# Second feed-forward network: an addition moved behind a maximum on the vector engine, and the next activations' load moved ahead of a weight load

## The chip, the cores and the metric

The kernel runs on one core of a Trainium2 chip. A core has a matrix engine (TensorE; PE in the profile, with its weight loads as PEld), a vector engine (VectorE, DVE), a scalar engine (ScalarE, ACT), a general engine (GpSimd, POOL) and a queue that here only issues DMAs (SyncE, SP). The engines run side by side, each in its own program order, and wait for one another by semaphores. The metric is the device time of one execution in microseconds; the profile covers one such execution.

## The reference, cut to what matters

```python
def reference(u, v, z, moe_w_in, moe_w_out, moe2_w_in, moe2_w_out):
    scores = (1 / S) * z @ z.T                       # B = 2, S = 3008, z: 64 wide
    x = u * (np.maximum(scores, 0) ** 2 @ v)         # 6016 tokens, 256 wide
    h = x @ moe_w_in                                 # first network, 256 -> 2048
    x = (h - np.tanh(h)) @ moe_w_out                 # 2048 -> 256
    h = x @ moe2_w_in                                # second network, 256 -> 2048
    g = np.where(h >= 1, h, np.where(h <= -1, 0.0, (h + 1) ** 2 / 4))
    return g @ moe2_w_out                            # 2048 -> 256
```

All is in float32. The kernel splits each operand into a rounded high part and a low rest, and makes a product from three products of such parts.

## The kernel before

The attention comes first and takes about 480 us of the span. Then come the two networks. Tokens are taken in **supertiles** of 1024 (the sixth has 896), the hidden width in 8 slices of 256. One supertile with one slice is a **unit**. The first network has 6 supertiles, so 48 units; the second has 5, so 40 units; its sixth supertile is done by other code at the end (lines 1043 on). Units run one after the other; `f` is the slice, 0 to 7.

A unit (class `Unit`, method `emit`) multiplies activations by input weights in a seven-product scheme for 2 x 2 blocks: `mult` puts three matmuls of 512 columns for each product into one of three PSUM banks, Y, X and V. ScalarE copies banks to SBUF (`snap`: m1, u2, u3), VectorE adds a copy and a bank (`add`). There are two halves, A and B, each of 128 x 1024 values. The first values of half A are m1 + X (in the trace `ha<-m,m`), the second u3 + V (`ha<-u,m`); half B gets a copy (`hb<-m`) and u2 + V (`hb<-u,m`).

Each half of the second network then goes through five steps: `first` clips to -1 and 1 (VectorE, line 519), `square` makes ((t + 1) / 2) squared (ScalarE, line 524), `value` takes the maximum of that and h (VectorE, line 527), `round` makes the high part `gha` or `ghb` (ScalarE, line 501), `rest` makes the low part `gla` or `glb` (VectorE, line 538). The matmuls with the output weights (line 584, `acc<-gha`, `acc<-ghb`, ...) need them. They belong to the unit before, `p`: `emit` interleaves the end of `p` with the start of the present unit. In program order, VectorE does, in a unit of the second network: `first` of p's half B, `rest` of p's half A, the addition m1 + X, `value` of p's half B, one fill, `rest` of p's half B, the addition u3 + V, `first` of half A, one fill, `value` of half A, the addition u2 + V. ScalarE does: m1 copy, `round` of p's A, `square` of p's B, u2 copy, `round` of p's B, the fill's rounding, u3 copy, `square` of A, the copy for half B.

A **fill** is one piece of side work from the list `fills`: preparing the next supertile's activations (`x_steps`, lines 441, 460 and 476), or turning results for output (line 705). A unit takes two. In the second network the units with f = 1 and 2 take four turns, those with f = 3 to 6 the eight preparation steps, and f = 7 and 0 find nothing; in its first supertile there are no turns yet and the preparation lies in f = 2 to 5.

`p.late` is true for every unit of the second network and for the very first unit of the first network, whose first half is rounded one unit later.

The order of the work is the order in which the code is written; no scheduler changes it. All loads go through one queue, SP, which issues in program order and waits at each issue for the buffer's release. `load_w(i + 2)` asks for a unit's weights (three DMAs of 512 KB) two units ahead, into a ring of 24 slots. `load_x` asks for the next supertile's activations (two DMAs of 512 KB into the two buffers `xr`), in the unit with f = 1, behind that unit's weights; the preparation steps are put into `fills` in the unit with f = 2.

Of the kernel before, what the change touches and what calls it, by code (L numbers as in the profile page):

```python
# [29 lines left out]
def attention_then_two_ffn(  # L30
# [60 lines left out]
    def flush():  # L91
        for fn in deferred:
            fn()
        deferred.clear()
# [314 lines left out]
    def load_w(i):  # L409

        if i < len(units):
            net, _, f = units[i]
        else:
            net, f = 1, i - len(units)
            if f >= NPF:
                return
        assert {(net, f, "in"), (net, f, "out")} <= done
        got = []
        for part in range(3):
            w = ring.tile([P, 1024], F32R, tag="w", name=f"w{i}_{part}")  # L420
            nc.sync.dma_start(out=w.bitcast(F32), in_=packed[net, f][:, part, :])
            got.append(w)
        ws[i] = [w.rearrange("p (n f) -> p n f", f=P) for w in got[:2]], got[2].rearrange("p (h j d) -> p h j d", h=2, j=2)
# [67 lines left out]
    def fill():  # L491

        if fills:
            for fn in fills.pop(0):
                if fn is not None:
                    fn()
        else:
            work(CONVERT[1])

    def copy(out_, in_):  # L500
        nc.scalar.activation(out=out_, in_=in_, func=AF.Copy)  # L501

    def add(out_, x, bank):
        nc.vector.tensor_tensor(out=out_, in0=x, in1=bank, op=ALU.add)  # L504
# [46 lines left out]
    class Unit:  # L551
# [59 lines left out]
        def emit(self, p, att=None):  # L611

            w = self.w
            before = p and p.net == 1 and p.f == 0 and p.s and p.before
            self.before = p
            self.late = self.net == 1 or att is not None
            one, two, three = p.parts_list if p else ([], [], [])
            Y = self.bank()
            self.mult(Y, A11, "b11", True)
            m1 = self.snap("m1", Y)  # L620
            if p and p.late:
                p.A.round()
            X = self.bank()
            self.mult(X, A12, "b21", True)
            if p:
                if p.net == 1:
                    p.B.first()
                p.A.rest()
                p.B.first() if p.net == 0 else p.B.square()
            self.A = Half(self.net, w, "a")  # L630
            add(self.A.h[:, 0, :w], m1, X[:, :w])
            V = self.bank()
            self.mult(V, S1, "t1", True)
            self.mult(Y, S2, "t2")
            u2 = self.snap("u2", Y)
            if before:
                before.empty(1)
            if p:
                p.B.value()
            for fn in one[:4] if before else one:  # L640
                fn()
            if att:
                att[0]()
            if p:
                p.B.round()
                fill()
                p.B.rest()
            self.mult(Y, S3, "t3")
            for fn in one[4:] if before else ():
                fn()  # L650
            u3 = self.snap("u3", Y)
            add(self.A.h[:, 1, :w], u3, V[:, :w])
            if self.net == 1 or att:
                self.A.first()
            for fn in two:
                fn()
            if att:
                att[1]()
            if not att:
                fill()  # L660
            if self.net == 1:
                self.A.square()
            self.mult(Y, A22, "t4")
            self.mult(V, S4, "b22")
            self.B = Half(self.net, w, "b")
            if self.net == 0 and not att:
                self.A.first()
            copy(self.B.h[:, 1, :w], Y[:, :w])
            self.A.value()
            if att:  # L670
                flush()
            add(self.B.h[:, 0, :w], u2, V[:, :w])
            for fn in three:
                fn()
            if not self.late:
                self.A.round()
            if p:
                p.empty(0)
            self.parts_list = self.parts()
# [32 lines left out]
    def split_steps():  # L712


        st = {}

        def load():
            for n, size in enumerate(SIZES):
                st[n] = u_p.tile([P, 2, 512], F32, tag="ub", name=f"xe{n}")
                nc.sync.dma_start(out=st[n][:, :, :size], in_=kept[1, LAST][:, :, n * QT : n * QT + size])  # L720

        def hi(n):
            def step():
                xsp[n] = [ring.tile([P, 2, 512], F32R, tag="w", name=f"xe{n}_{i}") for i in range(2)]
                copy(xsp[n][0][:, :, : SIZES[n]], st[n][:, :, : SIZES[n]])

            return step

        def lo(n):
            def step():  # L730
                s = (slice(None), slice(None), slice(0, SIZES[n]))
                nc.vector.tensor_tensor(
                    out=xsp[n][1][s], in0=st[n][s], in1=xsp[n][0].bitcast(F32)[s], op=ALU.subtract
                )

            return step

        return load, [(None, hi(0)), (lo(0), hi(1)), (lo(1), None)]
# [145 lines left out]
    with tc.manual_schedule():  # L884
# [79 lines left out]
        def second(i):  # L964
            if i >= LAG:
                _, av_fn, args = pairs[i - LAG]
                av_fn(*args, *held.pop(i - LAG))
# [50 lines left out]

        p = None
        for i, (net, s, f) in enumerate(units):  # L1020
            if i:
                load_w(i + 2)
            if f == 1:
                more = (net, s + 1) if (net, s + 1, 0) in units else (1, 0) if net == 0 else None
                load_x, steps = x_steps(*more) if more else split_steps()
                load_x()
            elif f == 2:
                fills.extend(steps)
            u = Unit(i)
            u.emit(p, att=(lambda: second(NATT), lambda: second(NATT + 1)) if i == 0 else None)  # L1030
            p = u
# [63 lines left out]
```

## Time and profile before

| What | Before |
|---|---|
| median of 3 runs | 1488.02 us (1487.14 to 1489.27) |
| the profiled execution | 1488.3 us, of which its span 1486.5 us |
| PE busy | 1465.1 us, 99% of the span |
| PEld busy | 1239.5 us, 83% |
| DVE busy | 1270.3 us, 85% |
| ACT busy | 1024.5 us, 69% |
| granted TensorE clock | 0.999 of full speed |

The table is to be read with care: PE's busy time is a modelled one, since matmuls overlap each other, and a share over the whole span mixes the attention with the two networks. The networks have to be looked at by stage and by unit.

### The profile page before, as it was taken

Reading aid. Unit: us, or ns where it says so; the run is one execution under the profiler, and the core shown is the slowest. Engines: PE = TensorE matmul, PEld = TensorE weight load, DVE = VectorE, ACT = ScalarE, POOL = GpSimd, SP = SyncE. Lnnn points to the kernel's source line nnn. Section 1 sums busy time; section 2 is a strip of 40 time slices with the busy share of each in tenths; the row PEclk is TensorE's granted clock in tenths of the full one; section 3 lists DMA queues with packets and bytes.
Section 4 is the critical chain, followed back from the end, with each engine's and each line's share of the span. In section 5 each row is a group of like instructions: output and inputs, shape, how many; then the busy total and the mean of one; then the engine's idle time right before and its main releaser. Section 6 shows DMA issues by size and latency. Waiting matters only on the chain.

```text
span 1486.5 us, 22226 instructions
## 1 busy us (share of the span) xinstructions
PE 1465.1 (99%) x8653; PEld 1239.5 (83%) x8653; DVE 1270.3 (85%) x1511; ACT 1024.5 (69%) x1249; POOL 55.5 (4%) x69
## 2 busy tenths in 40 slices
PE   9999999999999999999999999999999999999998
PEld 6888899999988788888888888977777777777897
DVE  8999888989988789898989888888788888887775
ACT  8877778977777676777666766665666666666543
POOL 0110000000110000000000000000000000000000
PEclk9999999999999999999999999999999999999999
DMA  6333235323345648374665757472564644456361
GB/s 156 87 100 97 82 99 116 79 82 100 100 128 166 228 133 306 138 256 162 234 258 189 275 184 271 154 279 90 176 203 170 198 163 134 150 171 215 128 198 26
DMA packets 202170, 240.81 MB, mean 162 GB/s; under 512 B 130000, under 2 KB 139088, under 8 KB 202064
## 3 DMA queue, kind: packets, MB, share of 16 engines
q1 hardware_dynamic: 200864, 239.12, 49.2%
q8 instruction: 68, 1.11, 0.3%
q10 hardware_dynamic: 1200, 0.26, 0.1%
q14 instruction: 38, 0.31, 0.1%
HBM read 195.69 MB, written 43.65 MB: 161 GB/s over the span
## 4 chain that ended last, share of the span: by engine, by line
PE 79%; DVE 9%; ACT 9%; issue 1%; DMA 1%; SPq 0%; ACTq 0%; DVEq 0%
PE acc L584 24%; PE acc L335 24%; PE m L565 20%; PE sc L287 6%; DVE gla L538 3%; DVE tb L527 3%; PE h L750 3%; ACT ghb L501 3%; ACT gha L501 3%; DVE ha L504 2%; ACT m L501 2%; PE acc L786 1%; PE acc L807 1%; DMA xr<-kept 1%; DVE glb L538 0%
## 5 line engine op out<-in xcount | busy, mean ns | idle before, releaser
L335 PE MATMUL acc<-hi,v 64*128 64x512 f32 (+1 forms) x2256 | 283.8, 383 | 0.0
L335 PEld LDWEIGHTS acc<-hi,v 64*128 64x128 f32 x2256 | 231.3, 184 | 24.0 <-ACT hi L300 0.8
L565 PE MATMUL m<-xht,w 128*128 128x512 f32 (+1 forms) x704 | 215.8, 388 | 0.0
L584 PE MATMUL acc<-ghb,w 128*128 128x512 f32 (+1 forms) x704 | 192.3, 395 | 10.4 <-ACT ghb L501 10.4
L308 ACT ACTIVATE r<-sc 128x1024 f32<-128x1024 f32 (+1 forms) x143 | 143.6, 1004 | 72.1 <-PE sc L287 71.6
L321 DVE TENSOR_TENSOR lo<-a,hi 128x1024 fp32r<-128x1024 f32 (+1 forms) x143 | 171.6, 1207 | 19.9 <-ACT a L315 17.3
L584 PE MATMUL acc<-gha,w 128*128 128x512 f32 (+1 forms) x704 | 173.4, 388 | 0.0
L584 PEld LDWEIGHTS acc<-ghb,w 128*128 128x128 f32 x704 | 129.1, 188 | 50.6 <-ACT ghb L501 26.7
L335 PE MATMUL acc<-lo,v 64*128 64x512 f32 (+1 forms) x1104 | 155.0, 383 | 1.7 <-DVE lo L321 1.7
L584 PEld LDWEIGHTS acc<-gha,w 128*128 128x128 f32 x704 | 132.1, 188 | 26.4 <-ACT gha L501 0.4
L565 PEld LDWEIGHTS m<-xht,w 128*128 128x128 f32 x704 | 132.3, 188 | 25.2
L311 ACT ACTIVATE hi<-r 128x1024 fp32r<-128x1024 f32 (+1 forms) x143 | 149.2, 1044 | 4.2
L501 ACT ACTIVATE ghb<-tb 128x1024 fp32r<-128x1024 f32 (+1 forms) x88 | 92.5, 1052 | 74.7 <-DVE tb L527 74.5
L527 DVE TENSOR_TENSOR ta<-ha,ta 128x1024 f32<-128x1024 f32 (+1 forms) x88 | 106.7, 1212 | 42.0 <-ACT ta L524 28.8
L565 PE MATMUL m<-xlt,w 128*128 128x512 f32 (+1 forms) x352 | 138.2, 392 | 0.6
L538 DVE TENSOR_TENSOR glb<-tb,ghb 128x1024 fp32r<-128x1024 f32 (+1 forms) x88 | 106.9, 1215 | 33.0 <-ACT ghb L501 32.5
L538 DVE TENSOR_TENSOR gla<-ta,gha 128x1024 fp32r<-128x1024 f32 (+1 forms) x88 | 106.8, 1213 | 32.5 <-ACT gha L501 32.0
L317 DVE TENSOR_TENSOR a<-r 128x1024 f32<-128x1024 f32 (+1 forms) x95 | 114.9, 1209 | 21.2 <-ACT r L308 19.1
L501 ACT ACTIVATE u<-m 128x512 f32<-128x512 f32 (+1 forms) x176 | 102.7, 583 | 33.9 <-PE m L565 32.9
L335 PEld LDWEIGHTS acc<-lo,v 64*128 64x128 f32 x1104 | 114.1, 184 | 14.2 <-DVE lo L321 3.2
L527 DVE TENSOR_TENSOR tb<-hb,tb 128x1024 f32<-128x1024 f32 (+1 forms) x88 | 106.4, 1209 | 4.2 <-ACT tb L517 0.2
L565 PE MATMUL m<-xhb,w 128*128 128x512 f32 (+1 forms) x352 | 107.7, 387 | 0.0
(103 smaller groups left out, 2333.0 us busy)
## 6 DMA issues: line engine op xcount, KB each, us to landing
w<-packed SPq DMA_DIRECT2D x288, 512.0 KB, 5.9
xr<-kept SPq DMA_DIRECT2D x20, 512.0 KB, 7.9
widein<-in_moe_w_in_dram SPq DMA_DIRECT2D x16, 512.0 KB, 5.5
wideout<-in_moe_w_out_dram SPq DMA_DIRECT2D x16, 512.0 KB, 4.4
packed<-phin SPq DMA_DIRECT2D x16, 512.0 KB, 2.9
packed<-plin SPq DMA_DIRECT2D x16, 512.0 KB, 2.9
vraw<-in_v_dram SPq DMA_DIRECT2D x22, 256.0 KB, 3.7
out_dram<-ot SPq DMA_DIRECT2D x88, 64.0 KB, 1.9
```

Source lines behind the costliest of these rows:

```text
L287: nc.tensor.matmul(ps[:, j, :n], zs[b, g][half, x, k0 : k0 + P], q[half, y, :n], start=(k == 0), stop=(k == 2))
L308: nc.scalar.activation(out=r[s], in_=ps[s], func=AF.Relu)
L311: nc.scalar.activation(out=hi[s], in_=r[s], func=AF.Square)
L317: nc.vector.tensor_tensor(out=a[s], in0=r[s], in1=r[s], op=ALU.mult)
L321: tail.append(lambda: nc.vector.tensor_tensor(out=lo[s], in0=a[s], in1=hi.bitcast(F32)[s], op=ALU.subtract))
L335: nc.tensor.matmul(acc[d][h][:, :n], lhsT, g[half, j, :n], start=start, stop=stop)
L501: nc.scalar.activation(out=out_, in_=in_, func=AF.Copy)
L527: nc.vector.tensor_tensor(out=self.t[self.s], in0=self.h[self.s], in1=self.t[self.s], op=ALU.subtract if self.net == 0 else ALU.max,)
L538: nc.vector.tensor_tensor(out=self.lo[self.s], in0=self.t[self.s], in1=self.hi.bitcast(F32)[self.s], op=ALU.subtract)
L565: nc.tensor.matmul(bank[:, : self.w], self.win[wp][:, block, :], xop[self.net, self.s][x][xp], start=start and i == 0, stop=True, skip_gro ...
L584: nc.tensor.matmul(self.acc(d, n)[:, : self.w], self.wout[:, part, j, d * P : (d + 1) * P], g[:, at, : self.w], start=start, stop=stop,)
L750: nc.tensor.matmul(banks[j][:, :n], win[wp][:, 2 * k + j, :], x[:, k, :n], start=(k == 0 and i == 0), stop=(k == 1 and i == 2),)
```

## The change

The addition m1 + X is issued behind `value` of p's half B whenever `p.late` holds, which is in all units of the second network but its first, and in the second unit of the first network. And `load_x` is called in the unit with f = 0, ahead of `load_w(i + 2)`, and no longer with f = 1 behind it; the preparation steps still enter `fills` with f = 2.

```diff
             self.A = Half(self.net, w, "a")
-            add(self.A.h[:, 0, :w], m1, X[:, :w])
+            if not (p and p.late):
+                add(self.A.h[:, 0, :w], m1, X[:, :w])
             V = self.bank()
...
             if p:
                 p.B.value()
+                if p.late:
+                    add(self.A.h[:, 0, :w], m1, X[:, :w])
             for fn in one[:4] if before else one:
...
         for i, (net, s, f) in enumerate(units):
-            if i:
-                load_w(i + 2)
-            if f == 1:
+            if f == 0:
                 more = (net, s + 1) if (net, s + 1, 0) in units else (1, 0) if net == 0 else None
                 load_x, steps = x_steps(*more) if more else split_steps()
                 load_x()
-            elif f == 2:
+            if i:
+                load_w(i + 2)
+            if f == 2:
                 fills.extend(steps)
```

On VectorE, in a unit of the second network without fills, there stood before (`tb<-hb,tb` is the maximum of half B, `ha<-m_` the addition m1 + X, `ha<-u_` the addition u3 + V):

```order
L538 TENSOR_TENSOR gla<-ta,gha 128x1024
L504 TENSOR_TENSOR ha<-m_12289,m 128x512
L527 TENSOR_TENSOR tb<-hb,tb 128x1024
L538 TENSOR_TENSOR glb<-tb,ghb 128x1024
L504 TENSOR_TENSOR ha<-u_12329,m 128x512
```

and stands now:

```order
L538 TENSOR_TENSOR gla<-ta,gha 128x1024
L527 TENSOR_TENSOR tb<-hb,tb 128x1024
L504 TENSOR_TENSOR ha<-m_12289,m 128x512
L538 TENSOR_TENSOR glb<-tb,ghb 128x1024
L504 TENSOR_TENSOR ha<-u_12329,m 128x512
```

The addition and the maximum have changed places; nothing else moves on VectorE, and the orders on TensorE and ScalarE stay as they were.

On SP, around the load of the second network's first activations (`xr_0_...<-kept_0_102`), there stood before (`w_..<-packed_2`, `packed_3`: the weights of the units f = 2 and f = 3; `kept_4`: results of the first network; `packed_6`: weights that the kernel converts on the way):

```order
L421 DMA w_0_10221<-packed_2_110 128x1024
L421 DMA w_1_10223<-packed_2_110 128x1024
L421 DMA w_2_10225<-packed_2_110 128x1024
L239 DMA packed_6_122<-phin_6_10197 128x1024
L239 DMA packed_6_122<-plin_6_10263 128x1024
L695 DMA kept_4_106<-y_10314 128x512
L695 DMA kept_4_106<-y_10317 128x512
```

five more issues down (two results, three weights of f = 3) came `xr`; and now there stands:

```order
L190 DMA widein_7_10176<-in_moe_w_in_dram 128x2x512
L435 DMA xr_0_0_10221<-kept_0_102 128x2x512
L435 DMA xr_0_1_10222<-kept_0_102 128x2x512
L421 DMA w_0_10225<-packed_2_110 128x1024
L421 DMA w_1_10227<-packed_2_110 128x1024
L421 DMA w_2_10229<-packed_2_110 128x1024
L239 DMA packed_6_122<-phin_6_10197 128x1024
```

The two activation loads have passed twelve issues: two of converted weights, four of results, and the weights of f = 2 and f = 3.

## Rows read from the trace of the kernel before

**Rows 1.** Busy time by stretch: start:end, us, PE (x), PEld, DVE, ACT, POOL
```profile
562.00:644.00 82.00, 82.00 (x363) 67.93 (x362) 72.70 (x88) 58.15 (x74) 2.87 (x4) 1.00 0.64 229
1052.00:1139.00 87.00, 84.89 (x363) 66.72 (x363) 73.31 (x85) 54.23 (x74) 0.00 (x0) 1.00 0.53 170
```

**Rows 2.** Chain that ended last, in order of time: start us, us, work
```profile
1066.35 3.37 PE acc L584 x14
1153.01 3.37 PE acc L584 x14
```

**Rows 3.** Waits of PE and PEld, 970 to 1395 us: us, times, longest
```profile
PE acc L584 <- ACT ghb L501: 9.9, 35, 0.3
PEld acc L584 <- ACT ghb L501: 25.8, 39, 0.7
PEld m L565 <- ACT u L501: 4.8, 17, 0.5
```

**Rows 4.** Timeline, first network, ScalarE's m1 copies: start us, us, engine, line
```profile
839.61 0.60 ACT L501 ACTIVATE m<-m 128x512 f32<-128x512 f32 x1 [0.81 <-PE m L565]
849.81 0.60 ACT L501 ACTIVATE m<-m 128x512 f32<-128x512 f32 x1 [0.80 <-PE m L565]
```

**Rows 5.** Timeline, second network, a unit without fills
```profile
1138.23 0.60 ACT L501 ACTIVATE m<-m 128x512 f32<-128x512 f32 x1 [0.92 <-PE m L565]
...
1139.67 1.05 ACT L524 ACTIVATE tb<-tb 128x1024 f32<-128x1024 f32 x1
...
1140.95 0.68 DVE L504 TENSOR_TENSOR ha<-m,m 128x512 f32<-128x512 f32 x1
1141.55 1.22 DVE L527 TENSOR_TENSOR tb<-hb,tb 128x1024 f32<-128x1024 f32 x1
...
1142.80 1.06 ACT L501 ACTIVATE ghb<-tb 128x1024 fp32r<-128x1024 f32 x1 [1.59 <-DVE tb L527]
...
1143.89 1.23 DVE L538 TENSOR_TENSOR glb<-tb,ghb 128x1024 fp32r<-128x1024 f32 x1 [1.13 <-ACT ghb L501]
1143.91 1.23 PEld L584 LDWEIGHTS acc<-ghb,w 128*128 128x128 f32 x6 [0.70 <-ACT ghb L501]
...
1149.02 0.60 ACT L501 ACTIVATE m<-m 128x512 f32<-128x512 f32 x1
```

**Rows 6.** Timeline, second network, a unit with fills
```profile
1099.31 1.22 DVE L476 TENSOR_TENSOR xlb<-xr,xhb 128x1024 fp32r<-128x1024 f32 x1
...
1100.52 1.23 DVE L538 TENSOR_TENSOR glb<-tb,ghb 128x1024 fp32r<-128x1024 f32 x1
...
1101.35 0.57 ACT L501 ACTIVATE u<-m 128x512 f32<-128x512 f32 x1
...
1101.95 0.69 DVE L504 TENSOR_TENSOR ha<-u,m 128x512 f32<-128x512 f32 x1 [0.20 <-ACT u L501]
...
1102.69 0.53 PEld L565 LDWEIGHTS m<-xhc,w 128*128 128x128 f32 x3 [0.19 <-DVE ha L504]
...
1105.75 0.60 ACT L501 ACTIVATE m<-m 128x512 f32<-128x512 f32 x1 [0.74 <-PE m L565]
```

**Rows 7.** Timeline, last supertile of the first network, f = 0 to 2
```profile
880.63 4.17 SPq L421 DMA_DIRECT2D w<-packed  x3
...
903.99 1.44 SPq L435 DMA_DIRECT2D xr<-kept  x2
...
915.23 0.69 DVE L441 TENSOR_TENSOR t<-xr,xr 128x512 f32<-128x512 f32 x1 [3.11 <-DMA xr<-kept]
...
917.51 0.88 PE L565 MATMUL m<-xhc,w 128*128 128x448 f32 x3 [1.12 <-DVE ha L504]
```

**Rows 8.** DMA issues: names, count, KB each, median us to landing
```profile
w<-packed SPq DMA_DIRECT2D x288, 512.0 KB, 5.9
xr<-kept SPq DMA_DIRECT2D x20, 512.0 KB, 7.9
```

**Rows 9.** Timeline, second unit of the first network
```profile
497.43 1.65 PE L584 MATMUL acc<-ghb,w 128*128 128x512 f32 x6 [0.44 <-ACT ghb L501]
```

## The prediction

> **What bounds the kernel now.** I began with the busy time by stretch [rows 1]. In both stretches TensorE does 363 matmuls, the work of eight units. In the first network this takes 82.00 us, in the second 87.00. So the second network loses 5 us in eight units, though TensorE looks busy for 84.89 of its 87.00 us. The chain that ended last gives the same unit more exactly: its steps in the second network stand 86.66 us apart (1066.35, 1153.01), which is 10.83 us a unit [rows 2]. In the first network, ScalarE's m1 copies stand 10.20 us apart [rows 4], with VectorE and ScalarE no less busy. I take 10.20 us as TensorE's own time for a unit and the other 0.63 as waiting.
>
> A rule of the Trainium skill bears on this reading (Perfetto Trace Analysis, Identifying the Most-Contended Engine): a matmul busy share is no measure of the distance to the bound, since matmuls overlap; the share of weight loads is better. The rows agree: the weight loads fill 67.93 of 82.00 us but 66.72 of 87.00. By the matmul share alone no more than 2.1 us in eight units could be won; by the count of matmuls, 5.0.
>
> What TensorE waits for is next [rows 3]. Nearly all of it is ghb, the rounded high part of half B: the weight loads wait for it 39 times in that stretch, 25.8 us, and the matmuls 9.9 us. Behind that comes a smaller wait for the u copy. The timeline of a unit without fills shows the chain [rows 5]. The square of half B is done at 1140.72 (1139.67 + 1.05). VectorE, free from gla, then does the addition m1 + X at 1140.95 and only at 1141.55 the maximum; 1.25 us later ghb starts, and 1.11 us after that TensorE loads the weights, having stood idle for 0.70 us. The m1 copy of the next unit comes 10.79 us after the last one. The chain runs round: m1 copy, gha, gla, addition, maximum, ghb, TensorE, next m1 copy. It, not TensorE, sets 10.79 us.
>
> **The addition moved, in 39 units.** These are the second network's units but the first. Without the addition before it, the maximum can start where the addition started, 1140.95: the square is over 0.23 us before. So maximum, ghb and weight load come 0.60 us sooner (1141.55 - 1140.95), and 0.10 of the 0.70 us is left. That much is hidden, as the weight loads run ahead of the matmuls. The chain is then 10.79 - 0.60 = 10.19 us, and TensorE's own 10.20 takes over by a hair: about 0.60 us a unit.
>
> The addition costs its 0.60 us behind the maximum, but there VectorE stood idle for 1.13 us, waiting for ghb, before glb [rows 5]. Its result is read by the clip of half A, which comes after the addition u3 + V. Bank X comes free some 1.2 us later; its next user is the V product of the following unit, some 6 us away. With that cover gone each tenth of a microsecond would cost 3.9 us in all.
>
> In a unit with fills [rows 6] the idle time is filled by a piece of preparation. If that is long (1.22 us at 1099.31), gla, maximum, addition, fill and glb run without a gap and glb stays at 1100.52. The addition u3 + V had waited 0.20 us for the u copy; the copy comes 0.60 sooner, so the addition can follow glb at 1101.66 (1100.52 + 1.14, the step from the maximum to the fill), not at 1101.95: 0.29 us sooner. The weight load that waits for it, at 1102.69, goes 0.29 us sooner too. So such a unit gains 0.29, not 0.60, and the wait for VectorE's ha is what is late next. There are two such units in each of four supertiles (the long pieces are the low parts of `b` and `t13`), eight in all. With a short piece (0.69 us) glb waits for ghb as before, and the gain is the full 0.60.
>
> Sum: 31 x 0.60 + 8 x 0.29 = 18.6 + 2.3 = 20.9 us. Bounds: all 39 units down to 10.20 give 39 x 0.63 = 24.6; if the 0.10 us of the weight load stays visible in each, 20.9 - 3.9 = 17.0.
>
> **The addition moved, in the second unit.** There the matmuls waited 0.44 us for ghb [rows 9], with the same addition ahead of the maximum. The end of the tanh, which takes the square's place, could bind as well, so the gain lies between 0 and 0.60; I take 0.4, near the wait itself.
>
> **The activations asked for sooner.** In the trace they cost time at one place, the last supertile of the first network [rows 7]. There SP issued the weights of f = 2 at 880.63, then waited for converted weights and results, and only at 903.99 asked for xr. VectorE waited 3.11 us for them, and TensorE 1.12 us for VectorE's addition, which stood behind. In the new order xr goes out at about 880.6, over 20 us sooner, and that wait is gone: 1.1 us. Its range is 0.9 to 1.4, as a late matmul also shows a weight load. At the other supertiles TensorE has no such wait, and I cost the move at nothing. What hides it there: the three weight loads now behind xr are asked for two units ahead, some 20 us [rows 4], and land in 5.9 us; even if they wait for all of xr, whose median is 7.9 [rows 8], this makes 13.8. Without that cover the price would be what is over 20 us, six times at most in each network. xr waits for nothing new on SP: its buffers were last read in the unit with f = 5 or 6. It passes twelve issues, each of which goes out later by xr's own issue, 1.44 us [rows 7], inside the same cover.
>
> **Sum.** 20.9 + 0.4 + 1.1 = 22.4 us. The profiled execution took 1488.3 us, so 1465.9; the median of the runs is 0.3 below that, so 1465.6. I say 1466 us. This case's own range is 1462 (24.6 + 0.6 + 1.4 = 26.6 off) to 1470 (17.0 + 0.9 = 17.9 off).
>
> **Rivals.**
>
> *A new wait in every unit.* If the u copy or the addition u3 + V ends late everywhere, as I reckon for eight units, each unit gains 0.29: 39 x 0.29 + 1.5 = 12.8 us, so 1475. For it speaks that VectorE would be busy nearly nine tenths of the time (73.31 of some 82 us), and that waits for the u copy are already there, 17 times [rows 3]. Against it: in units without fills VectorE has idle time before glb [rows 5].
>
> *Only the visible idle time comes back.* If 10.20 us cannot be reached because the matmuls simply run slower here, the gain is the matmuls' wait, 9.9 + 1.1 = 11 us: 1477. The equal work in 82 us [rows 1] speaks against it.
>
> *Another chain sets 10.8 us, or the maximum starts no sooner.* Then only the loads' 1.1 us remain: 1487. In nearly every unit the wait is put down to ghb, and ghb's to the maximum, so I give it little. That the change does not do what it says is excluded for the order, which is written out and shown above.
>
> *Slower: the maximum blocks the addition.* VectorE takes its work in order, so if the square ends late, the maximum holds up the addition, the fill and glb. This costs from the point where the square ends more than 0.83 us later than now against gla (the 0.23 to spare and the 0.60 won): at 1.2 us late, (1.2 - 0.83) x 39 = 14 us more, less 1.1: 1501. A page of the Trainium skill has the rule (TensorE: Matmul & The Clock Gate, Architectural detail): VectorE and ScalarE are strict first-in, first-out, so an operation that is ready gains nothing by standing behind one that waits. The trace has no row where the square is that late; the square follows gha on ScalarE at once, and gla needs gha as well, so both shift together. That speaks strongly against it.
>
> **How the numbers follow.** Forecast 0.66; a new wait everywhere 0.15; only the visible idle time 0.08; nothing but the loads 0.06; slower 0.05. The likeliest gives 1466. The range runs from 1462 to 1476, to take in the forecast and the first rival, 0.81 of the chance. About 0.2% (3 us) is what a measurement of this kernel can tell from no change: faster is the first three cases, 0.89; within it 0.06; slower 0.05.
>
> **What would show it.** In the changed kernel's timeline the maximum of half B should start where gla ends, the weight load's wait for ghb should shrink from 0.70 to about 0.1 us, and the m1 copies of the second network should stand 10.2 us apart without fills and some 10.6 in the eight long units, where a wait for ha or u is left. xr should be issued before the weights of f = 2, and VectorE's 3.11 us wait should be gone. I am wrong if the m1 copies stay at 10.8 us, if the maximum now waits for the square, or if TensorE waits for weights at f = 2.

## The result, and the profile after

| | Before | After |
|---|---|---|
| median of the runs | 1488.11 us (1487.14 to 1489.27) | 1469.16 us (1468.86 to 1469.92) |
| ratio after / before, 95% interval | | 0.9873 (0.9856 to 0.9890) |
| the profiled execution | 1488.3 us, span 1486.5 us | 1469.3 us, span 1467.5 us |

The change saves 18.95 us, 1.3%. Forecast were 1466 us in a range of 1462 to 1476, so direction, range and likeliest case held, and the gain came out 3.2 us short. The rest of this section finds where the time went.

The first row below is the page's busy time by engine; its columns are busy us, share of the span and number of instructions. The second is the share of the span of each engine in the chain that ended last.

```profile
PE 1457.0 (99%) x8653; PEld 1214.6 (83%) x8653; DVE 1268.1 (86%) x1511; ACT 1025.3 (70%) x1249; POOL 55.5 (4%) x69
...
PE 93%; ACT 3%; DVE 2%; DMA 1%; issue 0%; SPq 0%; ACTq 0%; DVEq 0%
```

The first row is nearly that of before: the same work, TensorE "99% busy" in both. The second has changed; before it was

```profile
PE 79%; DVE 9%; ACT 9%; issue 1%; DMA 1%; SPq 0%; ACTq 0%; DVEq 0%
```

So 93% of the chain is now TensorE's matmuls, where it was 79%, with 9% each for VectorE and ScalarE. The round over m1 copy, gha, gla, maximum and ghb no longer sets the time.

The busy time by stretch, after, over eight units of the second network (columns as in [rows 1]):

```profile
1047.98:1130.91 82.93, 82.81 (x361) 66.79 (x360) 72.46 (x85) 53.99 (x72) 0.00 (x0) 1.00 0.53 178
```

This stretch runs from one m1 copy to the eighth behind it, so it is eight units, 82.93 us. Before, eight units took 86.66 us in the second network [rows 2], and in the first they take 8 x 10.20 = 81.60 [rows 4]. (The stretches of [rows 1], 87.00 and 82.00 us, are cut at round times and hold 363 matmuls, three more than eight units.) So about three quarters of the difference between the two networks is gone, 3.73 of 5.06 us, and 1.33 us in eight units are left.

The chain in time order, after (start us, us, work), gives the same per unit:

```profile
1016.48 2.72 PE m L565 x12
...
1026.78 2.72 PE m L565 x12
...
1037.02 2.72 PE m L565 x12
```

Its steps stand 10.24 to 10.30 us apart, against 10.83 in [rows 2]. And they are steps of TensorE alone.

A unit without fills, the timeline after (start us, us, engine, line, operation, out<-in; in brackets the idle time ahead and what ended it), answers to [rows 5]:

```profile
1120.71 0.60 ACT L501 ACTIVATE m<-m 128x512 f32<-128x512 f32 x1 [0.74 <-PE m L565]
...
1122.18 1.07 ACT L524 ACTIVATE tb<-tb 128x1024 f32<-128x1024 f32 x1
1122.30 1.22 DVE L538 TENSOR_TENSOR gla<-ta,gha 128x1024 fp32r<-128x1024 f32 x1
...
1123.44 1.22 DVE L527 TENSOR_TENSOR tb<-hb,tb 128x1024 f32<-128x1024 f32 x1
...
1124.57 0.68 DVE L504 TENSOR_TENSOR ha<-m,m 128x512 f32<-128x512 f32 x1
...
1124.69 1.06 ACT L501 ACTIVATE ghb<-tb 128x1024 fp32r<-128x1024 f32 x1 [0.96 <-DVE tb L527]
...
1125.78 1.22 DVE L538 TENSOR_TENSOR glb<-tb,ghb 128x1024 fp32r<-128x1024 f32 x1 [0.53 <-ACT ghb L501]
1125.80 1.25 PEld L584 LDWEIGHTS acc<-ghb,w 128*128 128x128 f32 x6
...
1130.91 0.60 ACT L501 ACTIVATE m<-m 128x512 f32<-128x512 f32 x1 [0.94 <-PE m L565]
```

The maximum starts at 1123.44, straight behind gla; the square was done at 1123.25, so 0.19 us were to spare. The addition lies behind the maximum, inside the wait for ghb: VectorE's idle time ahead of glb went from 1.13 to 0.53 us, by just its 0.60. The weight load for ghb, which had waited 0.70 us, has no wait in its row. The next m1 copy comes 10.20 us after the last one, TensorE's own time for a unit [rows 4].

What is left of TensorE's waits in the second network, after (us in all, times, longest; the matmuls themselves have none), beside [rows 3]:

```profile
PEld m L565 <- DVE ha L504: 4.9, 17, 0.4
PEld m L565 <- ACT u L501: 4.3, 17, 0.5
```

and one more line of the same view of before:

```profile
PEld m L565 <- DVE ha L504: 2.5, 13, 0.2
```

The 25.8 us and 9.9 us for ghb are gone. The u wait is about as it was (4.8), and the wait for ha, the addition u3 + V, has grown from 2.5 to 4.9 us. The distances of the m1 copies show where these sit (taken from the starts as printed, so good to 0.01 us; the units with f = 1 and 2 have turns as fills):

| unit of the second network, supertiles 2 to 4 | us a unit, before | after |
|---|---|---|
| f = 0, 2, 7 | 10.77 to 10.80 | 10.20 to 10.24 |
| f = 3, 6 (short pieces of preparation) | 10.89 to 10.92 | 10.29 to 10.32 |
| f = 4, 5 (long pieces) | 10.78 to 10.90 | 10.50 to 10.55 |
| f = 1 | 10.82 | 10.64 |

The first three rows lost what the prediction gave them, about 0.58, 0.60 and 0.33 us a unit; f = 1 lost only 0.18.

Cut at the m1 copies, numbered 0 to 87, the two spans differ as follows; 19.0 us in all.

| stretch | before | after | difference |
|---|---|---|---|
| units 1 to 21 | 215.79 | 215.67 | -0.12 |
| unit 22 | 10.76 | 11.37 | +0.61 |
| units 23 to 40 | 183.13 | 183.09 | -0.04 |
| units 41 to 47 (last supertile, first network) | 65.27 | 64.84 | -0.43 |
| units 49 to 86 (second network) | 411.57 | 393.40 | -18.17 |
| unit 87 and the rest | 99.32 | 98.51 | -0.81 |

The addition's 39 units in the second network, with the code behind the last of them (the last row is not split further), account for 18.17 + 0.81 = 19.0 us, all of the gain. The earlier loads show 0.43 us, and unit 22 gives more than that back.

### The profile page after: what moved, and what is told of

Read it like the earlier page. It is cut to its first block, busy times and chain, and to the rows that moved or that the text cites. A ratio compares the mean times of both kernels' runs of the same rounds, so it can differ in the third digit from the quotient of the medians.

```text
span 1467.5 us, 22241 instructions
## 1 busy us (share of the span) xinstructions
PE 1457.0 (99%) x8653; PEld 1214.6 (83%) x8653; DVE 1268.1 (86%) x1511; ACT 1025.3 (70%) x1249; POOL 55.5 (4%) x69
## 4 chain that ended last, share of the span: by engine, by line
PE 93%; ACT 3%; DVE 2%; DMA 1%; issue 0%; SPq 0%; ACTq 0%; DVEq 0%
PE acc L584 30%; PE m L565 26%; PE acc L335 24%; PE sc L287 6%; PE h L753 3%; PE acc L789 1%; PE acc L810 1%; ACT gha L501 1%; DMA packed<-phin 1%; ACT m L501 0%; DVE glb L538 0%; DVE tb L527 0%; SPq L125 0%; ACT y L501 0%; ACT r L308 0%
## 5 line engine op out<-in xcount | busy, mean ns | idle before, releaser
L335 PEld LDWEIGHTS acc<-hi,v 64*128 64x128 f32 x2256 | 217.5, 184 | 37.9 <-ACT hi L300 0.8
L584 PE MATMUL acc<-ghb,w 128*128 128x512 f32 (+1 forms) x704 | 187.9, 389 | 0.0
L335 PEld LDWEIGHTS acc<-lo,v 64*128 64x128 f32 x1104 | 107.6, 184 | 20.9 <-DVE lo L321 3.2
```

Of the source, the lines that this page charges most:

```text
L335: nc.tensor.matmul(acc[d][h][:, :n], lhsT, g[half, j, :n], start=start, stop=stop)
L584: nc.tensor.matmul(self.acc(d, n)[:, : self.w], self.wout[:, part, j, d * P : (d + 1) * P], g[:, at, : self.w], start=start, stop=stop,)
```

## The experiments

**One part at a time.** First the addition alone, then the loads alone.

```diff
 # the addition alone (on after): the old calls again
-            if f == 0:
-                ... load_x()
             if i:
                 load_w(i + 2)
+            if f == 1:
+                ... load_x()
 # the loads alone (on before): the new calls, and the addition ahead of the maximum
```

> Only the addition is moved; the loads stay where they were before. Theory: the whole gain of 19 us comes from the addition in the second network, and the earlier loads brought nothing net, because the 1.1 us stall that they remove was followed in the trace of before by five units of 9.12 us, where the changed kernel has 9.30. So the span should be 1467 to 1468 us and the time 1469, the m1 copies of the last supertile of the first network should again show one unit of about 10.85 us and then units of 9.12, and 38 units of the second network should take 393 us as in the changed kernel. Rival (the prediction's sum): the loads are worth 1.1 us by themselves, so this kernel would take about 1470.3.

> Only the activations' load is moved; the addition stays ahead of the maximum. Theory: within 0.5 us of the kernel before (1488), since the stall of 1.1 us goes, but the units behind it take 9.30 us and no longer 9.12 (five of them, 0.9 us). Rival (the prediction's sum): 1.1 us faster, 1487.0, with units of 9.12 us all along. The second network's 38 units should stay at 411.6 us by both.

Measured: the addition alone 1469.24 us, ratio 0.9872 (0.9858 to 0.9885); the loads alone 1487.18 us, ratio 0.9990 (0.9981 to 0.9999). The addition alone takes units 49 to 86 from 411.57 to 393.35 us, after's 393.40; with the loads alone they stay at 411.46. So the whole gain in the second network is the addition's. The loads are worth about 1 us (1.29 by the medians of the loads alone) and not to be seen in the total here: 1469.24 against after's 1469.16. Both theories put down for the loads failed, that the units behind the stall would run at 9.12 us without the earlier loads and at 9.30 with them: with the addition alone they ran at 9.30, with the loads alone at 9.12. So the 1469 us expected of the addition alone came by another sum, and for the loads alone the rival came, the prediction's sum.

Where are they worth it? SP's issues in the last supertile of the first network, after:

```profile
881.03 1.20 SPq L435 DMA_DIRECT2D xr<-kept  x2
...
882.32 2.90 SPq L421 DMA_DIRECT2D w<-packed  x3
```

xr goes out ahead of the weights of f = 2, 23 us sooner than in [rows 7], and the first use of it on VectorE has no wait where 3.11 us stood:

```profile
912.45 0.68 DVE L441 TENSOR_TENSOR t<-xr,xr 128x512 f32<-128x512 f32 x1
```

But units 41 to 47 shortened by only 0.43 us. The m1 copies of after behind that place

```profile
919.33 0.55 ACT L501 ACTIVATE m<-m 128x448 f32<-128x448 f32 x1 [0.67 <-PE m L565]
928.63 0.55 ACT L501 ACTIVATE m<-m 128x448 f32<-128x448 f32 x1 [0.67 <-PE m L565]
```

stand 9.30 us apart, those of before

```profile
929.36 0.55 ACT L501 ACTIVATE m<-m 128x448 f32<-128x448 f32 x1
938.48 0.55 ACT L501 ACTIVATE m<-m 128x448 f32<-128x448 f32 x1 [0.73 <-PE m L565]
```

9.12 us. TensorE starts the 45 matmuls of such a unit 207 ns apart in the one and 203 ns in the other, at a granted clock of 1.00 in both. The loads alone ran at 9.12 without the stall:

```profile
909.65 0.55 ACT L501 ACTIVATE m<-m 128x448 f32<-128x448 f32 x1 [0.46 <-PE m L565]
918.77 0.55 ACT L501 ACTIVATE m<-m 128x448 f32<-128x448 f32 x1 [0.49 <-PE m L565]
```

and took 63.60 us for units 41 to 47. So the stall is worth over a microsecond, and the spacing of the matmuls about as much.

**Is the spacing a matter of the execution or of the program?** After and the addition alone were run once more, unaltered.

> The changed kernel once more, unaltered. In the profiles so far the 448-column matmuls of the first network's last supertile start either 207 ns apart (units of 9.30 us: the changed kernel, and the one with the addition alone) or 203 ns apart (units of 9.12 us: the loads alone, the version with the order at f = 1). Theory: which of the two comes is a matter of the execution and not of the program, so that one profile against another is uncertain by 5 to 6 x 0.18 = 1 us there; this profile may show either. Rival: it belongs to the program, and this one must show 9.30 again. Time 1469.2 by both.

> The addition alone once more, unaltered, on the same chip as the changed kernel. Theory: at equal spacing of the matmuls the late loads cost one stall of 1.1 us in the unit with f = 2 of the first network's last supertile, so that its seven units f = 1 to 7 take 1.1 to 1.3 us more than the changed kernel's at the same spacing, and the median is about 1.1 us above the changed kernel's, 1470.3. Rival: the loads are worth nothing, and the medians agree within 0.3 us.

Measured: after again 1468.53 us, ratio 0.9871 (0.9856 to 0.9886), units 41 to 47 in 64.84 us with 207 ns again; the addition alone again 1468.97 us, ratio 0.9873 (0.9857 to 0.9890), 65.82 us, 207 ns again. That speaks against a matter of the execution: both programs kept their spacing. The stall alone does not decide it either: before went from 207 to 203 ns across it, and the addition alone has the same stall and stayed at 207. What makes it is open. With programs of equal spacing the loads can be priced: 65.97 - 64.84 = 1.13 and 65.82 - 64.84 = 0.98 us. The pair of the two best versions below differs by 64.94 - 63.62 = 1.32 us; 0.15 us of it is unit 41, ahead of the stall, where the one with the old loads still ran at 207 ns and the other at 203, which leaves 1.17. That is the 1.1 us of the prediction. By medians the pairs give 1.29, 0.08, 0.84 and 0.44 us, each uncertain by some 0.5 to 1 us, so that the 1.1 us that were expected between the last two medians are neither shown nor excluded.

Unit 22 is no part of the change either. Its wait is that of ScalarE for a store (the timeline of after):

```profile
714.14 0.63 ACT L230 ACTIVATE phout<-wout 128x512 fp32r<-128x512 f32 x1 [2.40 <-DMA packed<-phin]
```

It took 11.37 us in after, 10.84 in after again, and between 10.39 and 11.07 in the other kernels.

**Why the addition gave 19.0 and not 20.9.** In the units with f = 1, TensorE loads weights as follows, and the other engines are at these works (timeline after):

```profile
1141.11 0.60 ACT L501 ACTIVATE m<-m 128x512 f32<-128x512 f32 x1
...
1142.95 1.07 PE L584 MATMUL acc<-gha,w 128*128 128x512 f32 x4
...
1143.50 0.59 ACT L501 ACTIVATE u<-m 128x512 f32<-128x512 f32 x1
...
1144.14 0.19 PEld L565 LDWEIGHTS m<-xlt,w 128*128 128x128 f32 x1 [0.54 <-ACT u L501]
...
1151.75 0.60 ACT L501 ACTIVATE m<-m 128x512 f32<-128x512 f32 x1 [1.37 <-PE m L565]
```

Only four gha matmuls stand ahead of the product that needs the bank of the u2 copy; elsewhere there are eight (`x8` in a unit without fills). The u2 copy (`u<-m`) comes at 1143.50, behind the square on ScalarE, too late for four, and TensorE waits 0.54 us. The m1 copies are 10.64 us apart. The same wait stood in the kernel before, where it was among the 17 of [rows 3]:

```profile
1152.05 0.19 PEld L565 LDWEIGHTS m<-xlt,w 128*128 128x128 f32 x1 [0.54 <-ACT u L501]
```

There it only took from the wait for ghb that followed; with that gone, it shows. In a long unit, after, the prediction's two waits are found:

```profile
1095.90 0.19 PEld L565 LDWEIGHTS m<-xlt,w 128*128 128x128 f32 x1 [0.15 <-ACT u L501]
...
1096.85 0.53 PEld L565 LDWEIGHTS m<-xhc,w 128*128 128x128 f32 x3 [0.39 <-DVE ha L504]
```

Two kernels take away one of these each: the fill ahead of glb is issued behind half A's clip instead, and in units with f = 1 the first two of the remaining output products go ahead of the product that waits.

```diff
 # the later fill (on after)
                 p.B.round()
-                fill()
+                if self.net == 0:
+                    fill()
                 p.B.rest()
 ...
             self.A.first()
+            if self.net == 1:
+                fill()
 # the other order at f = 1 (on after)
+            if before:
+                for fn in two[:2]:
+                    fn()
+                two = two[2:]
             self.mult(Y, S3, "t3")
```

> The changed kernel, and in the second network the first fill of a unit is issued behind the clip of half A and no longer between the rounding of half B and its low part. Theory: what is left above 10.20 us in the units with f = 3 to 6 (10.3 and 10.5 us) is the fill's work standing ahead of glb and of the u copy, so those 16 or so units come down to 10.2 to 10.25 and the kernel to about 1466 (8 x 0.30 + 8 x 0.08 = 3.0 us). Rival: VectorE's own work, 10.26 us in a unit with two long pieces, is the bound, so the time stays above 10.4 us there wherever the fill stands, and the kernel stays at 1469.

> The changed kernel, and in the four units with f = 1 that empty a bank of the supertile before, two matmuls with gla are issued ahead of the S3 product. Theory: these units take 10.63 us and not 10.2 because S3 waits 0.54 us for the u2 copy, with only four matmuls between S2 and S3; two more matmuls (0.45 us) cover it, so 10.63 goes to about 10.25 and the kernel gains 4 x 0.4 = 1.6 us, to 1467.6. Rival: gla is not ready that early, so TensorE waits for VectorE instead and the kernel stays at 1469.

Measured, the later fill: 1466.58 us, ratio 0.9854 (0.9841 to 0.9868), units 49 to 86 in 390.98 us, 2.4 less than after. The long units of supertiles 2 to 4 come 10.23 to 10.28 us apart. TensorE's waits, columns as above:

```profile
PEld acc L584 <- ACT ghb L501: 2.5, 12, 0.2
PEld m L565 <- ACT u L501: 2.2, 4, 0.5
```

The wait for ha is gone and the four u waits of f = 1 remain; 12 waits for ghb of at most 0.2 us are new. As VectorE does the same work, it is not the amount of its work that bounds the long units but the fill's place ahead of glb. The other order at f = 1: 1467.44 us, ratio 0.9860 (0.9846 to 0.9873). Its f = 1 units come 10.44 to 10.49 us apart, 0.15 to 0.20 less, not the whole 0.44 above TensorE's own time: the u wait is gone, but gla now comes too late:

```profile
1142.10 0.30 PEld L584 LDWEIGHTS acc<-gla,w 128*128 128x128 f32 x2 [0.37 <-DVE gla L538]
```

So theory and rival both held in part. Units 49 to 86 took 392.52 us, 0.9 less than after. The last supertile of the first network, which the edit does not touch, ran at 203 ns (63.60 against 64.84 us); so the median, 1.7 us below after's, came close to the 1467.6 expected partly by luck.

**Both together,** with the loads as in after and with those of before:

```diff
 # both edits above, on after; and the same with the old calls of load_x and load_w
```

> The changed kernel with the later first fill and the two matmuls ahead of S3 at f = 1. Theory: both gains add up, since they lie in different units: 2.6 us and 0.6 us off 1469.2, so 1466, and 1.1 us less than its partner with the old loads. Rival: the gains overlap, and it is no faster than the one with the later fill alone, 1466.6.

> The moved addition, the later first fill and the two matmuls ahead of S3 at f = 1, but the activations' loads where they were before. Against the same kernel with the earlier loads, on the same chip. Theory: the earlier loads save the one stall of 1.1 us at the end of the first network, so this kernel is 1.1 us slower than its partner; each of the two makes some 3 us over the changed kernel's 1469 (2.6 by the later fill, 0.6 by the order at f = 1), so 1467 here and 1466 there. Rival: the loads are worth nothing once the addition is moved, as the first pair seemed to say, and both take the same.

Measured: with the new loads 1466.09 us, ratio 0.9857 (0.9842 to 0.9871), units 49 to 86 in 390.14 us; with the old ones 1466.93 us, ratio 0.9862 (0.9847 to 0.9876), 390.56 us. The first has the lowest median of all kernels, 3.1 us below after's; they were not timed side by side and the intervals of their ratios overlap, but in units 49 to 86, where both edits act, it is 3.3 us ahead, and 0.8 us ahead of the later fill alone, so the two gains add up there. Its m1 copies in long units are 10.23 us apart (ScalarE's timeline of this kernel):

```profile
1077.10 0.60 ACT L501 ACTIVATE m<-m 128x512 f32<-128x512 f32 x1 [0.94 <-PE m L565]
...
1087.33 0.60 ACT L501 ACTIVATE m<-m 128x512 f32<-128x512 f32 x1 [0.98 <-PE m L565]
```

38 units at 10.20 us would be 387.6; 2.5 us are left to win in this stretch.

**A later square.** The rival on the slower side lived on a late square. A copy of 448 columns, whose result nobody reads, stands ahead of the square on ScalarE:

```diff
+                if p.net == 1:
+                    copy(snap_p.tile([P, 448], F32, tag="spare", name="spare"), m1[:, :448])
                 p.B.first() if p.net == 0 else p.B.square()
```

> The changed kernel with one more copy on ScalarE (128 x 448, into a spare tile that nothing reads) ahead of half B's square in the second network, so that the square ends about 0.5 us later. Theory of the chain: the maximum had 0.23 us to spare and the weight load for ghb next to nothing, so the maximum starts some 0.25 us late and each of the 39 units grows by about that: 6 to 10 us more than the changed kernel, 1475 to 1479, with the maximum waiting for the square. Rival: ghb has slack by now and the copy is hidden, 1469 to 1470.

Measured: 1482.21 us, ratio 0.9963 (0.9950 to 0.9976). Units 49 to 86 took 406.50 us, 13.1 over after, 0.34 a unit; those without fills take 10.50 to 10.56 us. The timeline of this kernel, ScalarE and VectorE around the maximum:

```profile
1147.50 0.57 ACT L501 ACTIVATE spare<-m 128x448 f32<-128x448 f32 x1
...
1147.64 1.23 DVE L538 TENSOR_TENSOR gla<-ta,gha 128x1024 fp32r<-128x1024 f32 x1 [0.39 <-ACT gha L501]
...
1147.96 1.05 ACT L524 ACTIVATE tb<-tb 128x1024 f32<-128x1024 f32 x1
...
1149.05 1.22 DVE L527 TENSOR_TENSOR tb<-hb,tb 128x1024 f32<-128x1024 f32 x1 [0.19 <-ACT tb L524]
```

The waits, in us in all, times, longest:

```profile
DVE tb L527 <- ACT tb L524: 7.3, 39, 0.2
...
PEld acc L584 <- ACT ghb L501: 13.6, 35, 0.4
...
PEld m L565 <- ACT u L501: 8.5, 27, 1.0
```

The square starts 0.46 us (1147.96 - 1147.50) later than it would, and the maximum waits for it in each of 39 units. It now starts 1.41 us behind gla's start (1149.05 - 1147.64) and not 1.14 (1123.44 - 1122.30), so 0.27 us later: the 0.46 less the 0.19 to spare. More than that is lost, 13.1 us and not the 6 to 10 expected, since the copy also pushes the u copies back (8.5 us of waits instead of 4.3). So after has next to no room: TensorE's 10.20 us and the chain's 10.19, by the prediction's working, lie so close that most of any delay shows.

**The addition twice.** The moved addition is done a second time, in the second network alone, to ask how much cover it has:

```diff
-                    add(self.A.h[:, 0, :w], m1, X[:, :w])
+                    for _ in range(2 if self.net == 1 else 1):
+                        add(self.A.h[:, 0, :w], m1, X[:, :w])
```

> The changed kernel with the moved addition issued twice in the second network (the second writes the same values), which is 0.60 us more on VectorE in 39 units. Theory: in its new place the addition lies in VectorE's wait for ghb. In the units without fills some 0.5 us of that wait is left, so they stay at 10.2 us; in the eight units with a long piece ahead of glb the whole 0.60 shows, in those with a short piece about a third to a half of it: 8 x 0.6 + 16 x 0.25 = 9 us more, 1478. Rival: there is no cover there, and the kernel loses 39 x 0.60 = 23 us, 1492.

Measured: 1481.14 us, ratio 0.9956 (0.9940 to 0.9973), units 49 to 86 in 405.30 us, 11.9 over after. The timeline of a unit without fills has the two additions and then glb, with no idle time and no loss (10.20 to 10.23 us a unit):

```profile
1129.58 1.40 DVE L504 TENSOR_TENSOR ha<-m,m 128x512 f32<-128x512 f32 x2
...
1129.69 1.06 ACT L501 ACTIVATE ghb<-tb 128x1024 fp32r<-128x1024 f32 x1 [0.97 <-DVE tb L527]
...
1130.90 1.22 DVE L538 TENSOR_TENSOR glb<-tb,ghb 128x1024 fp32r<-128x1024 f32 x1
```

Units with short pieces took 10.70 to 10.72 us, 0.4 more than in after, long ones 11.23 to 11.25, 0.7 more; with f = 2, where the fills are turns, 0.4 to 0.65 were lost, and with f = 1 under 0.1. Expected were 9 us in all, from 0.6 in the long units and 0.25 in the short ones, so both were put too low. TensorE's waits of this kernel:

```profile
PEld m L565 <- DVE ha L504: 18.1, 26, 1.2
```

So the cover for the moved addition is the wait ahead of glb, and it is there only in units whose fill does not use it already. A page of the Trainium skill has the rule behind it (TensorE: Matmul & The Clock Gate, Architectural detail): VectorE and ScalarE work strictly first-in, first-out, so glb and u3 + V cannot pass the second addition. The trace agrees: ghb is done at 1130.75 (1129.69 + 1.06), but glb starts only where the second addition ends, at 1130.90.

## Why the prediction was right, and where it was short

- **What bounds the kernel.** Right. The unit's 10.20 us, taken from the first network, is what units without fills now have. Over equal stretches of 340 us in the second network (1050 to 1390) before did 1416 matmuls and after 1482.
- **The addition in units without fills.** Right in mechanism and size. The maximum moved by 0.60 us to the end of gla, the wait for ghb went from 0.70 to none, and the addition disappeared in VectorE's wait ahead of glb. The 0.10 us that was argued to be hidden is hidden.
- **The eight long units.** Right: forecast was a unit of some 10.6 us with a wait for ha or u left, measured were 10.50 to 10.55 us, with 0.15 us for u and 0.39 for ha.
- **The units with f = 1: the step that failed.** The sum gave them the full 0.60, as it gave all that have no long piece. They gave 10.82 - 10.64 = 0.18 us, since the u wait of 0.54 us, seen as the "smaller wait" behind ghb and met in a rival, was not asked for its place. Four units lack 4 x 0.42 = 1.7 us. They stand in the term of 20.9 us, which measured 19.0, and are nearly all of what it fell short; the other 27 units gave some 0.03 less each than the 0.60, and the long ones some 0.03 more than the 0.29.
- **The second unit.** Forecast 0.4, measured 0.14 us. The maximum starts 0.46 us sooner behind the m1 copy, and the weight load's wait for ghb falls from 0.86 to 0.42 us, as it should. But then TensorE waits for ha, which it did not before (timeline after):

```profile
496.94 1.23 PEld L584 LDWEIGHTS acc<-ghb,w 128*128 128x128 f32 x6 [0.42 <-ACT ghb L501]
...
499.11 0.53 PEld L565 LDWEIGHTS m<-xhc,w 128*128 128x128 f32 x3 [0.26 <-DVE ha L504]
```

  The forecast looked at the wait and not at the work behind it on VectorE, which there also prepares weights: the addition u3 + V comes only 0.18 us sooner.
- **The loads.** Forecast 1.1 us; measured 0.98 to 1.17 us at equal matmul spacing. In this pair of kernels only 0.43 us of it are to be seen, as after runs the seven units behind at 9.30 us and not 9.12. No wait for weights appeared at f = 2, and the landing times stayed inside the cover of 20 us, the longest weight load with 11.7 us (the DMA view of after; names, count, KB each, median us):

```profile
w<-packed SPq DMA_DIRECT2D x288, 512.0 KB, 6.3
...
xr<-kept SPq DMA_DIRECT2D x20, 512.0 KB, 6.9
```

- **The rivals.** A new wait in every unit: such waits came, but cost something like the rival's price only in the eight long units and the four with f = 1. That only visible idle time comes back was refuted: the matmuls reached 10.20 us a unit, and the gain was 19 us where that case gives 11. That only the loads' 1.1 us remain was refuted by the addition alone, which took 18.2 us off units 49 to 86. The slower case did not come; the square had 0.19 us to spare. Its mechanism is real, and its price was too low: with the square 0.46 us later, of which 0.23 were to cost nothing, 0.23 us a unit should have been lost, and 0.34 were: 0.27 by the later maximum, the rest with the u copies that this kernel also delays. The deciding point was put at 0.83 us. By these numbers it lies nearer: the unit's gain of 18.17 / 38 = 0.48 us, less 0.34 at 0.46 us late, leaves 0.14, so that at about 0.6 us the change would have brought nothing, an estimate for a delay made in this way that takes every further tenth as paid in full.

With the f = 1 wait seen, the sum would have been 20.9 - 1.7 + 0.4 + 1.1 = 20.7 us and the forecast 1467.6 us for the profiled execution, which took 1469.3. The rest is the loads' part that the matmul spacing hid (0.7), unit 22 (0.6) and the second unit (0.3).

## What to carry to other kernels

Where a closed round over several engines sets the time, look for an operation in it that nobody in the round needs and that can lie inside a wait of its own engine further on; what it brings is its duration, down to the busiest engine's own time for the unit, which a stage with the same matmuls shows. Then list the waits of that engine that are hidden behind the one that goes: each of them comes back, in the units where it stands. Price a load's move in the stretch where it stands and not by the total, if other programs' matmul spacing or a store's wait shift by as much.

## What the runs showed of the hardware that was not expected

- **Matmuls of 448 columns ran at two spacings,** 203 and 207 ns, at a granted clock of 1.00 in both, for a whole supertile (9.12 and 9.30 us a unit, 1.2 us in all). Kernels with 203 are the loads alone, the other order at f = 1 and the best; before and the best with the old loads went from 207 to 203 across the stall; with 207 ran after, the addition alone, the later fill, the later square and the addition twice, and both programs run twice had 207 both times. The matmuls of 512 columns had 227 ns in all of them (10.20 us / 45). The cause is open.
- **The busy time of the weight loads is not a fixed yardstick.** The first lines of the view by line, for the weight loads of the attention's largest product, which the change doesn't touch, in after and in after again, which are the same program:

```profile
L335 PEld LDWEIGHTS acc<-hi,v 64*128 64x128 f32 x2256 | 217.5, 184 | 37.9 <-ACT hi L300 0.8 <-issue 0.7 <-DVE y L381 0.3
```

```profile
L335 PEld LDWEIGHTS acc<-hi,v 64*128 64x128 f32 x2256 | 223.7, 184 | 31.6 <-ACT hi L300 0.8 <-issue 0.7 <-DVE y L381 0.3
```

  As many loads of the same 184 ns make 217.5 us in one and 223.7 in the other, and 231.3 in before. The durations add up to 415 to 416 us (2256 x 184 ns) in all three: the busy time counts a moment once however many loads overlap in it, so it moves with their overlap. The prediction's reading by weight loads agreed with the count of matmuls in its two stretches, but the count is the firmer measure.
- **A wait seen in the trace is what is left after the waits ahead of it.** The u wait of 0.54 us at f = 1 had the same length in both kernels, and cost nothing in one and some 0.4 us in the other.
